# Storing L in halves, sharing its tiles between short steps, packing the last pair's right sides, and loading two weight pieces apart

## The chip, the cores and the metric

One core of a Trainium2 chip runs the whole program: TensorE (PE) multiplies, VectorE (DVE) and ScalarE (ACT) do elementwise work, SyncE (SP) issues most transfers and ACT the rest. The metric is the device time of one execution in microseconds; less is better.

## The reference

```python
# attention: 8 x 8 heads, 576 positions of 64, in two steps through 32 packed rows
p_packed = sm_attn(p, k, v)
x = sm_attn(q, p_packed, p_packed)          # as 4608 tokens x 512
# first block
a = x @ w1; b = x @ w2                      # 512 -> 1024
x = (a * b @ w3) @ w_out                    # -> 512
# second block
h = x @ w_in                                # 512 -> 2048
g = where(h >= 1, h, where(h <= -1, 0.0, (h + 1) ** 2 / 4))
return g @ w_out                            # -> 512
```

Everything is float32.

## The kernel before, in words

Attention and the first block fill the first 588 us. They leave x, transposed, in DRAM. The change touches what follows, the second block.

**Products.** A float32 factor is split into a high part and a rest, and a product is three passes: high times high, high times rest, rest times high. Both layers of the second block use a scheme with seven products of half blocks instead of eight. Its products are named A11, S1, S2, A12, S4, S3 and A22; each has its weights (`wi` tiles, or `ws` tiles for S4 and A22, the two in `STREAM`, which are loaded anew for each step) and its right side (`x2s` tiles, made from x by `x2_tasks`).

**Steps.** The first layer (line 999) has 40 steps `s`. The tokens go in five pairs of column blocks (`PAIRS`): four wide pairs of 2 x 512 tokens and a short one of 2 x 256. A pair has eight steps `i`, one for each 128 rows of a quarter of the weights. A step issues its products in the order A11, S1, S2, then A22 of the step before, then A12, S4, S3, six matrix products each (two row halves times three passes). They collect in three PSUM banks: A11, S2, S3 and A22 in x, S1 and S4 in z, A12 in y.

**What follows a product.** ACT copies the first sums out (`m1`, `m5`, `u2`, line 879). DVE adds them to later ones (line 883) and so makes the four quarters of h: two in a U tile, two in an L tile. The last of these adds, `L<-x,m`, reads bank x after S3; only then may A22 go on in that bank. The activation is three ACT instructions (816, 819) and a DVE one (822) for each quarter. `upper` treats U; `lower_begin`, `lower_relu` and `lower_middle` treat L, after A22. `upper_end` (849) and `lower_end` (872) form three differences in the third plane of U and the last two of L. Of U's three planes two are stored, in single pieces; of L's four planes (G21, G22, GT3, GT2) all, in one transfer of 1 MB (512 KB in the short pair). Stores are gathered in a list and issued by SP at the end of a step (`flush_stores`, 833). U and L have two tiles each, so a step's first write into a tile waits until the store of two steps before has landed.

**Right sides.** While a pair runs, `x2_tasks` makes the seven right sides of the next one, eleven tasks, dealt out over the steps by the tables `MID` and `LAST`. A task `parts` is one ACT instruction (678) and one DVE instruction (679); a task `combine` one DVE instruction (673). There are nine `x2s` tiles, so the third right side of the next pair takes the tile of this pair's A11, which is free only in step 7.

**Near the end of the layer** `first_sides` loads the first weights (`w`, `hwi`) and inputs (`raw`) of the second layer, through SP too. The second layer (line 1093) reads the stored planes back as `raw` or `r`, splits them into `op` tiles (967, 968) and multiplies (1102).

**Queues.** SP and ACT each issue their instructions in order. A transfer's landing is told by one of eight counters, which the program gives out in turn over both queues; a transfer that gets a counter first waits until the counter's previous transfer has landed.

Of the kernel before, what the change touches and what calls it, by code (L numbers as in the profile page):

```python
# [56 lines left out]
def fused_kernel(ctx: ExitStack, tc, qT, kT, vv, pb, w1, w2, w3T, wo, win, wout, out):  # L57
# [610 lines left out]
    def x2_tasks(t):  # L668

        N = PAIRS[t][1]  # L670

        def combine(dst, a, b):
            return lambda: nc.vector.tensor_tensor(out=x2f[dst], in0=x2f[a], in1=x2f[b], op=ALU.subtract)

        def parts(q, src):
            def f():
                x = x2_t[t, q] = late["b1"].tile([P, 2, 2, 512], F32R, name="x2s", tag="x2s", bufs=9)
                nc.scalar.activation(out=x[:, 0, :, :N], in_=x2f[src], func=AF.Copy)
                nc.vector.tensor_tensor(  # L679
                    out=x[:, 1, :, :N], in0=x2f[src], in1=x[:, 0, :, :N].bitcast(F32), op=ALU.subtract)  # L680
            return f
        return [
            parts(A11, 11), combine(11, 12, 11), combine(12, 22, 12), parts(S1, 11), combine(11, 22, 11),
            parts(S2, 11), parts(A12, 21), parts(S4, 22), parts(S3, 12), combine(11, 21, 11), parts(A22, 11),
        ]
# [66 lines left out]
    def ws_tile():  # L752
        return wp.tile([P, 2, 2, 2, P], F32R, name="ws", tag="ws", bufs=2)

    def ws_load(s, eng):
        if s < 8 * len(PAIRS):
            t = ws_t[s] = first.pop("ws", None) or ws_tile()
            eng.dma_start(out=t.bitcast(F32), in_=wst[s % 8 // 4][:, s % 4])
# [13 lines left out]
    first["ws"] = ws_tile()  # L772
# [5 lines left out]
    ws_load(0, nc.sync)  # L778
    for i in (S2, A12, S3):
        wi_load(i, 0)  # L780
    ws_load(1, nc.sync)
# [12 lines left out]
    def product(s, q):  # L794
# [7 lines left out]
        for k in range(2):  # L802
            for v, m in PASSES:
                if q in STREAM:
                    w = ws_t[s][:, STREAM.index(q), k, v, :]
# [55 lines left out]
    def lower_middle(s):  # L861
# [5 lines left out]
        smaller(h[:, 1, :N], h[:, 1, :N], r[:, 1])  # L867

    def lower_end(s):
# [5 lines left out]
        store(s, G21, 4, h[:, :, :N])  # L875
# [98 lines left out]
    LAST = {2: 2, 3: 1, 4: 1, 5: 1, 7: 2, 0: 1}  # L974

# [23 lines left out]
    for s in range(steps):  # L999
# [19 lines left out]
        if s:  # L1019
            product(s - 1, A22)  # L1020
            ws_load(s + 1, nc.scalar)
            lower_relu(s - 1)
            lower_middle(s - 1)
# [6 lines left out]
        tasks(MID.get(i, 0))  # L1030
        kept[s, 1] = buf("L")
        product(s, S4)
        add(kept[s, 0][:, 1, :N], bank.pop((s, "z")), u2, N)
        product(s, S3)
        add(kept[s, 1][:, 1, :N], bank[s, "x"], m5, N)
        tasks(LAST.get(i, 0))
        if s and not short:
            if i == 0:
                upper_end(s - 1)
            lower_end(s - 1)  # L1040
        flush_stores()
# [136 lines left out]
```

## Time and profile before

| | |
|---|---|
| median of 3 runs (lowest to highest) | 1317.23 us (1315.96 to 1319.09) |
| the profiled execution | 1317.88 us, its span 1316.1 us |
| PE busy | 1260.2 us, 96% |
| DVE busy | 878.0 us, 67% |
| ACT busy | 677.1 us, 51% |
| mean granted TensorE clock | 0.993 |
| DMA | 299.46 MB, mean 228 GB/s |

A share of 96% does not say that 4% is all there is to win: a product that waits in the middle of a group counts partly as busy, and the share is a mean over stages with different limits. The span is the profiler's; the device time has about 1.8 us more around it.

### The profile page before, as it was taken

Reading aid. Unit: us, or ns where it says so; the run is one execution under the profiler, and the core shown is the slowest. Engines: PE = TensorE matmul, PEld = TensorE weight load, DVE = VectorE, ACT = ScalarE, POOL = GpSimd, SP = SyncE. Lnnn points to the kernel's source line nnn. Section 1 sums busy time; section 2 is a strip of 40 time slices with the busy share of each in tenths; the row PEclk is TensorE's granted clock in tenths of the full one; section 3 lists DMA queues with packets and bytes.
Section 4 is the critical chain, followed back from the end, with each engine's and each line's share of the span. In section 5 each row is a group of like instructions: output and inputs, shape, how many; then the busy total and the mean of one; then the engine's idle time right before and its main releaser. Section 6 shows DMA issues by size and latency. Waiting matters only on the chain.

```text
span 1316.1 us, 21364 instructions
## 1 busy us (share of the span) xinstructions
PE 1260.2 (96%) x8312; PEld 1055.6 (80%) x8312; DVE 878.0 (67%) x1462; ACT 677.1 (51%) x1144; POOL 0.7 (0%) x6
## 2 busy tenths in 40 slices
PE   6989989999999999999999999998899999999998
PEld 2367788889888889997878877787877788888888
DVE  5975777778577768625778877877557646455464
ACT  3444344545445454525677666766557343434433
POOL 0000000000000000000000000000000000000000
PEclk9999999999999999999999999999999999999999
DMA  9771674637466542278667675766999957768675
GB/s 352 252 249 59 212 245 159 235 135 253 135 209 196 210 152 95 99 264 288 239 207 267 219 277 199 250 224 201 323 365 324 375 197 262 252 224 287 210 225 176
DMA packets 125397, 299.46 MB, mean 228 GB/s; under 512 B 10352, under 2 KB 53360, under 8 KB 120816
## 3 DMA queue, kind: packets, MB, share of 16 engines
q1 hardware_dynamic: 86352, 232.94, 50.7%
q10 hardware_dynamic: 38944, 65.16, 14.6%
q8 instruction: 65, 1.06, 0.4%
q14 instruction: 36, 0.29, 0.1%
HBM read 196.21 MB, written 101.84 MB: 226 GB/s over the span
## 4 chain that ended last, share of the span: by engine, by line
PE 63%; DVE 14%; DMA 14%; ACT 6%; issue 3%; ACTq 1%; SPq 0%; DVEq 0%
PE x L1102 13%; PE psk L405 12%; PE psk L381 9%; PE x L808 7%; PE z L1102 6%; DMA g<-L 6%; PE y L1102 4%; PE z L808 3%; PE psk L489 3%; PE y L808 2%; PE psk L181 2%; DMA wi<-hl 1%; DMA raw<-g 1%; DVE x2s L679 1%; DMA g<-U 1%
## 5 line engine op out<-in xcount | busy, mean ns | idle before, releaser
L381 PE MATMUL psk<-at,m 128*128 128x288 f32 x1494 | 213.1, 298 | 5.2 <-ACT ta L391 2.7
L405 PEld LDWEIGHTS psk<-g,w 128*128 128x128 f32 x1500 | 199.9, 188 | 20.4 <-ACT st L432 6.3
L381 PEld LDWEIGHTS psk<-at,m 128*128 128x128 f32 x1494 | 200.6, 188 | 17.8 <-issue 7.4
L405 PE MATMUL psk<-g,w 128*128 128x288 f32 x1500 | 206.2, 296 | 6.2 <-ACT st L432 2.8
L808 PE MATMUL x<-x2s,wi 128*128 128x512 f32 (+1 forms) x720 | 163.8, 372 | 2.9 <-ACT m L879 2.9
L808 PEld LDWEIGHTS x<-x2s,wi 128*128 128x128 f32 x720 | 127.0, 190 | 28.3 <-ACT m L879 4.6
L968 DVE TENSOR_TENSOR op<-raw,op 128x1024 fp32r<-128x1024 f32 (+1 forms) x94 | 101.8, 1114 | 69.5 <-ACT op L967 69.1
L967 ACT ACTIVATE op<-raw 128x1024 fp32r<-128x1024 f32 (+1 forms) x94 | 87.4, 966 | 70.9 <-DVE raw L959 32.5
L1102 PE MATMUL x<-op,w 128*128 128x512 f32 (+1 forms) x480 | 101.5, 371 | 1.4 <-DVE op L968 1.4
L1102 PE MATMUL x<-op,hwi 128*128 128x512 f32 (+1 forms) x480 | 100.9, 369 | 0.5 <-DVE op L968 0.5
L1102 PEld LDWEIGHTS x<-op,w 128*128 128x128 f32 x480 | 84.4, 190 | 17.8 <-DVE op L968 2.5
L1102 PEld LDWEIGHTS x<-op,hwi 128*128 128x128 f32 x480 | 82.9, 188 | 17.0 <-DVE op L968 1.3
L393 DVE TENSOR_TENSOR tb<-psk,ta 128x288 f32<-128x288 f32 x124 | 56.2, 453 | 57.8 <-ACT ta L391 36.0
L819 ACT ACTIVATE r<-r 128x1024 f32<-128x1024 f32 (+1 forms) x80 | 78.0, 975 | 2.5
L968 DVE TENSOR_TENSOR op<-r,op 128x1024 fp32r<-128x1024 f32 (+1 forms) x46 | 50.2, 1117 | 38.9 <-ACT op L967 38.7
L489 PE MATMUL psk<-wo,w3f 128*128 128x512 f32 x128 | 62.5, 641 | 11.6 <-DVE w3f L136 11.6
L879 ACT ACTIVATE m<-x 128x512 f32<-128x512 f32 (+1 forms) x40 | 22.1, 552 | 91.5 <-PE x L808 82.9
L125 ACT ACTIVATE cvt<-raw 128x512 f32<-128x512 f32 x72 | 48.3, 676 | 40.3 <-DMA raw<-w 10.7
L808 PE MATMUL x<-x2s,ws 128*128 128x512 f32 (+1 forms) x240 | 60.1, 384 | 9.3 <-DVE L L883 8.2
L391 ACT ACTIVATE ta<-psk 128x288 f32<-128x288 f32 x125 | 50.4, 403 | 28.3 <-PE psk L381 24.3
L967 ACT ACTIVATE op<-r 128x1024 fp32r<-128x1024 f32 (+1 forms) x46 | 43.2, 969 | 39.0 <-DVE L L1079 15.7
L489 PEld LDWEIGHTS psk<-wo,w3f 128*128 128x128 f32 x128 | 25.5, 207 | 44.1 <-issue 28.3
(118 smaller groups left out, 1898.7 us busy)
## 6 DMA issues: line engine op xcount, KB each, us to landing
raw<-g SPq DMA_DIRECT2D x86, 512.0 KB, 5.2
g<-L SPq DMA_DIRECT2D x32, 1024.0 KB, 6.3
r<-g SPq DMA_DIRECT2D x42, 512.0 KB, 5.2
ws<-ws ACTq DMA_DIRECT2D x38, 512.0 KB, 5.1
g<-U SPq DMA_DIRECT2D x64, 256.0 KB, 5.8
x2d<-st ACTq DMA_DIRECT2D x72, 144.0 KB, 2.1
v<-vv SPq DMA_DIRECT2D x8, 1280.0 KB, 7.3
wi<-hl ACTq DMA_DIRECT2D x20, 512.0 KB, 3.3
```

Source lines behind the costliest of these rows:

```text
L125: nc.scalar.activation(out=t, in_=raw.bitcast(F32).rearrange("p (n two) -> p n two", two=2)[:, :, 1], func=AF.Copy, scale=2.0 ** -112)
L181: nc.tensor.matmul(ps[r][NP * q:NP * q + NP], stat[64 * r:64 * r + 64, NP * q:NP * q + NP], mov(q)[64 * r:64 * r + 64], start=True, stop=True,
L381: nc.tensor.matmul(ps[w][:, :HS], m_tile[b, w, n][:, s, G, c0 * P:(c0 + 1) * P], at_tile[b][:, G, v, hf * HS:(hf + 1) * HS], start=(k == 0 ...
L391: nc.scalar.activation(out=bs, in_=ps[1][:, :HS], func=AF.Copy)
L393: nc.vector.tensor_tensor(out=g, in0=ps[0][:, :HS], in1=bs, op=ALU.mult)
L405: nc.tensor.matmul(ps, w34[kt][:, s, mt * P:(mt + 1) * P], g_t[kt, hf][:, v, :], start=(kt == kts[0] and n == 0), stop=(kt == kts[-1] and ...
L489: nc.tensor.matmul(acc[4 * hf + m], w3f[hf, j][:, m * P:(m + 1) * P], wof[j], start=(j == 0), stop=(j == 7))
L808: nc.tensor.matmul(bank[s, b][:, :N], w, x2_t[t, q][:, m, k, :N], start=(j == 0 and q in (A11, S1, A12)), stop=(j == 5), skip_group_check= ...
L819: nc.scalar.activation(out=r, in_=r, func=AF.Square)
L967: nc.scalar.activation(out=o[:, :, 0, :N], in_=a[0], func=AF.Copy)
L968: nc.vector.tensor_tensor(out=o[:, :, 1, :N], in0=a[0], in1=o[:, :, 0, :N].bitcast(F32), op=ALU.subtract)
L1102: nc.tensor.matmul(bank[b][d][:, :N], w2_t[q][j // 2][:, 2 * (j % 2) + k, s, d * P:(d + 1) * P], op[x][:, k, v, :N], start=start and k == ...
```

## The change

- `store`: L's first two planes (G21, G22) are stored when `lower_middle` has made them, and flushed there with U's stores; `lower_end` stores only the last two (GT3, GT2), named from GT3 on.
- L's tiles in the short pair: an even and an odd step share one tile of 512 columns.
- Right sides of the short pair: two share one `x2s` tile. While the fourth pair runs, its tasks are dealt out by `LAST_SHORT`, with none in the middle of a step.
- `lower_end` in step 7 of a pair goes ahead of the tasks.
- `ws`: one tile and load for S4's piece and one for A22's, 256 KB each instead of 512 KB for both. S4's is loaded by ACT two steps ahead, right after product S4; A22's by SP one step ahead, at the end of a step.

```diff
@@ -672,9 +672,19 @@
         def combine(dst, a, b):
             return lambda: nc.vector.tensor_tensor(out=x2f[dst], in0=x2f[a], in1=x2f[b], op=ALU.subtract)
 
+        room = []
+
         def parts(q, src):
             def f():
-                x = x2_t[t, q] = late["b1"].tile([P, 2, 2, 512], F32R, name="x2s", tag="x2s", bufs=9)
+                if not room:
+                    x = late["b1"].tile([P, 2, 2, 512], F32R, name="x2s", tag="x2s", bufs=9)
+                    if N == 512:
+                        room.append(x)
+                    else:
+                        x = x.rearrange("p a b (c n) -> p (a b c n)", n=N).rearrange(
+                            "p (o a b n) -> p o a b n", o=2, a=2, b=2)
+                        room.extend([x[:, 0], x[:, 1]])
+                x = x2_t[t, q] = room.pop(0)
                 nc.scalar.activation(out=x[:, 0, :, :N], in_=x2f[src], func=AF.Copy)
                 nc.vector.tensor_tensor(
                     out=x[:, 1, :, :N], in0=x2f[src], in1=x[:, 0, :, :N].bitcast(F32), op=ALU.subtract)
@@ -749,13 +759,13 @@
     def wi_load(i, n):
         nc.sync.dma_start(out=wi_t[i, n].bitcast(F32), in_=wid[i][n])
 
-    def ws_tile():
-        return wp.tile([P, 2, 2, 2, P], F32R, name="ws", tag="ws", bufs=2)
-
-    def ws_load(s, eng):
+    def ws_tile(x):
+        return wp.tile([P, 2, 2, P], F32R, name=f"ws{x}", tag=f"ws{x}", bufs=2)
+
+    def ws_load(s, x, eng):
         if s < 8 * len(PAIRS):
-            t = ws_t[s] = first.pop("ws", None) or ws_tile()
-            eng.dma_start(out=t.bitcast(F32), in_=wst[s % 8 // 4][:, s % 4])
+            t = ws_t[s, x] = first.pop(f"ws{x}", None) or ws_tile(x)
+            eng.dma_start(out=t.bitcast(F32), in_=wst[s % 8 // 4][:, s % 4, x])
 
 
     for tag in ("m1", "m5", "U", "u2"):
@@ -769,16 +779,18 @@
         wi_tile(i, 1, wp)
     for i in (S1, S2):
         wi_tile(i, 0, wp)
-    first["ws"] = ws_tile()
+    for x in range(2):
+        first[f"ws{x}"] = ws_tile(x)
     wi_tile(A12, 0, wq)
     wi_tile(S3, 0, wq)
     wi_tile(S3, 1, wo2)
     for i in (A11, S1):
         wi_load(i, 0)
-    ws_load(0, nc.sync)
+    ws_load(0, 0, nc.sync)
+    ws_load(0, 1, nc.sync)
     for i in (S2, A12, S3):
         wi_load(i, 0)
-    ws_load(1, nc.sync)
+    ws_load(1, 0, nc.sync)
 
 
     BANK = {A11: "x", S1: "z", A12: "y", S2: "x", S4: "z", S3: "x", A22: "x"}
@@ -802,7 +814,7 @@
         for k in range(2):
             for v, m in PASSES:
                 if q in STREAM:
-                    w = ws_t[s][:, STREAM.index(q), k, v, :]
+                    w = ws_t[s, STREAM.index(q)][:, k, v, :]
                 else:
                     w = wi_t[q, n][:, k, v, c0 * P:(c0 + 1) * P]
                 nc.tensor.matmul(
@@ -865,6 +877,8 @@
         square(r)
         smaller(h[:, 0, :N], ps, r[:, 0])
         smaller(h[:, 1, :N], h[:, 1, :N], r[:, 1])
+        store(s, G21, 2, h[:, :2, :N])
+        flush_stores()
 
     def lower_end(s):
         N = PAIRS[s // 8][1]
@@ -872,7 +886,7 @@
         nc.vector.tensor_tensor(
             out=h[:, 2:4, :N], in0=h[:, 1:2, :N].to_broadcast([P, 2, N]), in1=kept.pop((s, 0))[:, 1:3, :N],
             op=ALU.subtract)
-        store(s, G21, 4, h[:, :, :N])
+        store(s, GT3, 2, h[:, 2:4, :N])
 
     def copy(tag, ps, N):
         c = buf(tag)[:, :N]
@@ -972,6 +986,7 @@
 
     MID = {7: 1, 0: 1}
     LAST = {2: 2, 3: 1, 4: 1, 5: 1, 7: 2, 0: 1}
+    LAST_SHORT = {2: 2, 3: 2, 4: 1, 5: 1, 6: 1, 7: 2, 0: 1}
 
 
     def first_sides(s):
@@ -1018,7 +1033,6 @@
         u2 = copy("u2", bank[s, "x"], N)
         if s:
             product(s - 1, A22)
-            ws_load(s + 1, nc.scalar)
             lower_relu(s - 1)
             lower_middle(s - 1)
         product(s, A12)
@@ -1027,17 +1041,27 @@
         short = t + 1 == len(PAIRS) and i
         if short:
             lower_end(s - 1)
-        tasks(MID.get(i, 0))
-        kept[s, 1] = buf("L")
+        to_short = t + (i > 0) + 1 == len(PAIRS)
+        tasks(0 if to_short else MID.get(i, 0))
+        if t + 1 < len(PAIRS):
+            kept[s, 1] = buf("L")
+        else:
+            if s % 2 == 0:
+                both = buf("L")
+            kept[s, 1] = both[:, :, s % 2 * N:(s % 2 + 1) * N]
         product(s, S4)
+        ws_load(s + 2, 0, nc.scalar)
         add(kept[s, 0][:, 1, :N], bank.pop((s, "z")), u2, N)
         product(s, S3)
         add(kept[s, 1][:, 1, :N], bank[s, "x"], m5, N)
-        tasks(LAST.get(i, 0))
-        if s and not short:
+        if i == 7 and not short:
+            lower_end(s - 1)
+        tasks((LAST_SHORT if to_short else LAST).get(i, 0))
+        if s and i < 7 and not short:
             if i == 0:
                 upper_end(s - 1)
             lower_end(s - 1)
+        ws_load(s + 1, 1, nc.sync)
         flush_stores()
         for w in {0: (A11, S1), 1: (S2, A12, S3)}.get(s, ()):
             wi_load(w, 1)
```

The first place is SP's queue where the first layer begins: the loads for step 0 and 1, before the stores of step 0. `wi` with a number is one product's weights, in the order A11, S1, S2, A12, S3 for the first five; DMAHW0 to DMAHW7 are the eight counters. Before:

```order
L750 DMA wi_7300<-wi_60 128x2048 [waits DMAHW2_49,PE_49]
L750 DMA wi_7308<-wi_62 128x2048 [waits DMAHW3_49,PE_49]
L758 DMA ws<-ws_74 128x1024 [waits DMAHW4_49]
L750 DMA wi_7309<-wi_64 128x2048 [waits DMAHW5_49]
L750 DMA wi_7311<-wi_66 128x2048 [waits DMAHW7_49,DMAHW6_49]
L750 DMA wi_7312<-wi_70 128x2048 [waits DMAHW7_49,PE_49]
L758 DMA ws<-ws_74 128x1024 [waits DMAHW0_49]
L750 DMA wi_7301<-wi_61 128x2048 [waits DMAHW1_49]
```

and now:

```order
L760 DMA wi_7300<-wi_60 128x2048 [waits DMAHW2_49,PE_49]
L760 DMA wi_7308<-wi_62 128x2048 [waits DMAHW3_49,PE_49]
L768 DMA ws_7310<-ws_74 128x512 [waits DMAHW4_49]
L768 DMA ws_7311<-ws_74 128x512 [waits DMAHW5_49]
L760 DMA wi_7309<-wi_64 128x2048 [waits DMAHW6_49]
L760 DMA wi_7312<-wi_66 128x2048 [waits DMAHW7_49]
L760 DMA wi_7313<-wi_70 128x2048 [waits DMAHW0_49,PE_49]
L768 DMA ws_7322<-ws_74 128x512 [waits DMAHW1_49]
L768 DMA ws_7371<-ws_74 128x512 [waits DMAHW2_49]
```

The load for S3, the fifth `wi`, moved from counter 7 to counter 0, and the loads behind it one on as well.

The second place is the same queue in the short pair, where step 36 and the first stores of step 37 stand. `U` and `L` rows are stores, `w` and `raw` are loads for the second layer. Before:

```order
L833 DMA g_87<-U 128x256 [waits DMAHW1_49,DVE_49]
L833 DMA g_87<-U 128x256 [waits DMAHW2_49,DVE_49]
L833 DMA g_87<-L 128x4x256 [waits DMAHW3_49,DVE_49]
L917 DMA w_9919<-w_76 128x512 [waits DMAHW4_49]
L950 DMA raw_10150<-g_83 128x1024 [waits DMAHW5_49,PE_49]
L833 DMA g_87<-U 128x256 [waits DMAHW7_49,DVE_49]
L833 DMA g_87<-U 128x256 [waits DMAHW0_49,DVE_49]
```

and now:

```order
L845 DMA g_87<-U 128x256 [waits DMAHW1_49,DVE_49]
L845 DMA g_87<-U 128x256 [waits DMAHW2_49,DVE_49]
L845 DMA g_87<-L 128x2x256 [waits DMAHW4_49,DVE_49]
L768 DMA ws_10251<-ws_75 128x512 [waits DMAHW5_49,PE_49]
L845 DMA g_87<-L 128x2x256 [waits DMAHW6_49,DVE_49]
L931 DMA w_10020<-w_76 128x512 [waits DMAHW7_49]
L964 DMA raw_10259<-g_83 128x1024 [waits DMAHW0_49]
L845 DMA g_87<-U 128x256 [waits DMAHW2_49,DVE_49]
L845 DMA g_87<-U 128x256 [waits DMAHW3_49,DVE_49]
```

A step has seven transfers on SP where it had five; with ACT's one `ws` load these are eight and six. The second `L` row of a step is the half that `lower_end` makes.

The third place is DVE in the short pair, from the middle of step 32's activation to the add that ends step 33. `L<-x,m` is that add, the one that A22 waits for. Before:

```order
L822 SCALAR_TENSOR_TENSOR U<-U,r 128x256
L849 TENSOR_TENSOR U<-U 128x256 [waits DVE_49]
L822 SCALAR_TENSOR_TENSOR L<-x,r 128x256 [waits Activation_49]
L822 SCALAR_TENSOR_TENSOR L<-L,r 128x256
L883 TENSOR_TENSOR U<-y,m_9852 128x256 [waits DMAHW7_49,DMAHW6_49,PE_49]
L872 TENSOR_TENSOR L<-L,U 128x2x256 [waits DVE_49]
L883 TENSOR_TENSOR U<-z,u_9877 128x256 [waits PE_49]
L883 TENSOR_TENSOR L<-x,m_9869 128x256 [waits DMAHW0_49,PE_49]
```

and now:

```order
L834 SCALAR_TENSOR_TENSOR U<-U,r 128x256
L861 TENSOR_TENSOR U<-U 128x256 [waits DVE_49]
L834 SCALAR_TENSOR_TENSOR L<-x,r 128x256 [waits Activation_49]
L834 SCALAR_TENSOR_TENSOR L<-L,r 128x256
L897 TENSOR_TENSOR U<-y,m_9951 128x256 [waits DMAHW6_49,DMAHW2_49,PE_49]
L886 TENSOR_TENSOR L<-L,U 128x2x256 [waits DVE_49]
L897 TENSOR_TENSOR U<-z,u_9976 128x256 [waits PE_49]
L897 TENSOR_TENSOR L<-x,m_9968 128x256 [waits PE_49]
```

The order of these rows is the same; the add has lost its wait for counter 0, since step 33 writes into the tile that step 32 took.

## Rows read from the trace of the kernel before

**Rows 1.** The chain that ended last, shares by engine.
```profile
PE 63%; DVE 14%; DMA 14%; ACT 6%; issue 3%; ACTq 1%; SPq 0%; DVEq 0%
```

**Rows 2.** That chain by time: start, duration, what; 740 to 890 us.
```profile
747.89 2.35 DVE x2s L679 x2
...
751.40 7.00 DMA g<-L
...
771.55 8.48 DMA g<-L
...
878.18 2.75 PE x L808 x12
```

**Rows 3.** Waits: total, times, longest; 588 to 904, then 904 to 962.
```profile
DVE L L883 <- DMA g<-L: 32.0, 16, 3.2
...
DVE L L883 <- DMA g<-L: 7.5, 3, 3.8
```

**Rows 4.** PE's timeline: start, duration, tile, count; 586 to 985 us.
```profile
589.85 1.54 PE L808 MATMUL z<-x2s,wi 128*128 128x512 f32 x6
...
904.82 0.86 PE L808 MATMUL z<-x2s,wi 128*128 128x256 f32 x6
...
946.72 0.87 PE L808 MATMUL z<-x2s,wi 128*128 128x256 f32 x6
947.42 0.90 PE L808 MATMUL x<-x2s,wi 128*128 128x256 f32 x6
...
962.02 11.94 PE L1102 MATMUL x<-op,w 128*128 128x512 f32 x48
```

**Rows 5.** Windows: busy times, then granted clock, DMA's busy share, GB/s.
```profile
904.10:920.00 15.90, 12.00 (x76) 10.84 (x75) 12.64 (x23) 10.03 (x18) 0.00 (x0) 0.88 0.45 146
920.00:962.00 42.00, 35.53 (x269) 34.16 (x269) 25.49 (x63) 24.77 (x52) 0.00 (x0) 0.95 0.98 326
962.00:1000.00 38.00, 37.36 (x159) 29.70 (x158) 23.08 (x27) 22.99 (x32) 0.00 (x0) 0.98 0.99 346
```

**Rows 6.** Transfers issued from 904 to 962: count, KB, median us to landing.
```profile
g<-L SPq DMA_DIRECT2D x7, 512.0 KB, 5.6
g<-L SPq DMA_DIRECT2D x2, 1024.0 KB, 7.1
...
g<-U SPq DMA_DIRECT2D x14, 128.0 KB, 6.9
```

**Rows 7.** SP's waits and timeline, 570 to 600, and PE's first S3.
```profile
SPq L758 <- DMA x2d<-st: 9.9, 2, 9.5
...
594.45 0.32 SPq L758 DMA_DIRECT2D ws<-ws  x1
...
596.03 3.00 PE L808 MATMUL x<-x2s,wi 128*128 128x512 f32 x12
```

**Rows 8.** PE and DVE's timeline in the short pair; in brackets the idle time before.
```profile
912.76 0.42 DVE L883 TENSOR_TENSOR U<-z,u 128x256 f32<-128x256 f32 x1
...
913.83 0.98 PE L808 MATMUL x<-x2s,wi 128*128 128x256 f32 x6 [2.15 <-ACT m L879]
...
916.36 2.04 PE L808 MATMUL x<-x2s,ws 128*128 128x256 f32 x6 [1.55 <-DVE L L883]
...
951.80 0.94 PE L808 MATMUL z<-x2s,ws 128*128 128x256 f32 x6 [2.06 <-DMA ws<-ws]
...
952.39 0.43 DVE L883 TENSOR_TENSOR U<-y,m 128x256 f32<-128x256 f32 x1 [0.60 <-DMA g<-U]
...
960.57 1.65 PE L808 MATMUL x<-x2s,ws 128*128 128x256 f32 x6 [2.14 <-DVE L L883]
```

**Rows 9.** SP's waits from 904 to 962.1.
```profile
SPq L833 <- DMA raw<-g: 3.1, 2, 2.1
```

**Rows 10.** The chain that ended last, 962 to 1000 us.
```profile
970.15 10.63 DMA raw<-g
...
988.88 8.49 PE x L1102 x35
```

## The prediction, made before the changed kernel was run

> **What bounds the kernel now.** I read the chain that ended last first: matrix products hold 63% of the span, and DVE and DMA share 14% each [rows 1]. The chain by time then shows where the DMA share sits in the stage that the change touches (588 to 962 us): pieces named "DMA g<-L" of 7 to 8.5 us, each the store of an L tile that a later step wants back [rows 2]. The waits say what stands behind them: DVE's add into L (line 883) sat 32.0 us in 16 waits for that store in the four wide pairs, and 7.5 us in 3 waits in the short pair [rows 3]. PE feels it, because the product A22 goes into the bank that this add must first read.
>
> How much PE loses comes from starts. Twelve matrix products take 2.75 us [rows 2], so one group of six takes 1.375; from S1 of step 0 at 589.85 to S1 of step 32 at 904.82 there are 222 wide groups and a narrow one, 305.9 us, and 315.0 passed: 9.0 us lost in the wide pairs [rows 4]. A narrow group takes 947.42 - 946.72 = 0.70 [rows 4]; from 904.82 to the last stage's first product at 962.02 stand one wide and 55 narrow groups, 39.9 us, and 57.2 passed: 17.3 us lost in the short pair. So 26 us is all that this stage can give.
>
> The windows add the other limit: DMA was busy 0.45 of the time from 904 to 920, then 0.98 to 962 and 0.99 to 1000 [rows 5]. Work that gets faster there meets transfers that do not.
>
> **The sum, against the profiled execution.** It took 1317.88 us (span 1316.1 and 1.8 around it), 0.65 over the median of the runs, 1317.23; I subtract from the median, since the terms are differences.
>
> *L in halves, wide pairs: -6.0.* G21 and G22 leave about half a step earlier; what the add waits for is the second half, issued where the whole tile was, but 512 KB. The nearest rows are those of the short pair: an L of 512 KB landed after 5.6 us, one of 1024 KB after 7.1 [rows 6]. That is 1.5 us per wait directly, and more in a row of waits, since a late add makes the next store late ([rows 2]: the store issued at 751.40, with the right-side work of 747.89 ahead of it, led to the one at 771.55). At step 7 of a pair the change also puts lower_end ahead of that right-side work, 2.35 us earlier for two DVE instructions [rows 2]. The upper bound is the whole 9.0. From the rows: PE lost 9.0 for 32.0 waited, 0.28 of each; 16 waits shorter by 1.5 are 24 us, times 0.28 is 6.7. Some of the 9.0 is right-side work at a pair's border, which stays. The lower bound, 3.0, is that half as many waits are long enough to matter. I take 6.0.
>
> *The start: +1.2.* The order of SP's queue shows that cutting the first ws load in two moves every later load to the next counter. The load for S3, which had counter 7, now has counter 0, where the store of an x2 piece was pending: the ws load that stood there waited 9.5 us, until 594.45, while S3's first product began at 596.03 [rows 7]. A 1 MB load issued at 594.45 cannot be there at 596.03. With S3's megabyte out of the way the store should land one to two us sooner, and the load takes some 4 to 5 us; the stall is 0 to 3.0, and I take 1.2. The loads queued behind it are used a step later or more.
>
> *The short pair: -8.3.* (a) Step 32's z sum into U ran at 912.76, 0.42 long, so its add into L could have ended at 913.6; A22 began at 916.36 [rows 8]. The add waited for step 30's store, whose second half now leaves ahead of the border's right-side work and is half as large: -2.7. (b) The other two waits of the 7.5 [rows 3] are 4.8 us. Odd short steps wait for no store of L any more, as the order shows, and even ones for stores two steps older; DVE has slack for part of the wait, so -2.0. (c) Granted clock was 0.88 of full from 904 to 920 and 0.95 from 920 to 962 [rows 5], 1.9 and 2.1 us lost if PE had been busy throughout: a stretch at the lower level, 1.2 GHz, right after the idle 2.15 and 1.55 us of [rows 8]. With those two idles shortened I expect most of it back; at three quarters busy, -2.9 (bounds 0 and -4.0). (d) ws of S4 is now loaded two steps ahead. The wait of 2.06 at 951.80 goes; but U's y sum waited for its own store until 952.39 [rows 8], just as late, so I count three quarters of it, -1.5. (e) Right sides packed by twos need four tiles instead of seven, so A12's no longer waits for step 31; no instruction is added, and what it saves lies in the DVE work ahead of the add, which (a) already counts. (f) Each short step from 36 on issues eight transfers instead of six, and there are eight counters. SP already stood 3.1 us for a counter whose load had not landed [rows 9]: +0.8. The wait at the end, 2.14 before A22 at 960.57 [rows 8], is a chain of DVE work with no next step to cover it, and stays.
>
> *The last stage: +2.0.* Its first products are gated by loads: one was 10.63 us under way, and PE stood at 988.88 [rows 10]. DMA was full from 920. If it is filled from 904 on, those loads can come earlier by at most 0.55 x 15.9 + 0.02 x 42 = 9.6 us [rows 5]; the early short steps can't issue that much, so I take two thirds, 6.3. What PE gained beyond that, 8.3 - 6.3, is given back (bounds 0 and 4).
>
> Edits at no cost: A22's ws piece on SP stands where PE's use of the old one is a step past; on ACT the S4 load waits for product S4, when ACT's next work needs the product after it anyhow. If a counter is late there, ACT's copy m1 and then PE's S2 wait.
>
> Sum: -6.0 + 1.2 - 8.3 + 2.0 = **-11.1**, from 1317.2 to **1306.1 us**.
>
> **A rule against it.** The three kinds of store in [rows 6] were under way 7 x 5.6 + 2 x 7.1 + 14 x 6.9 = 150 us inside 58: they overlap, so a transfer's fixed part is not paid by its neighbours. The stretch with mostly small ones ran at 326 GB/s, the next one at 346 with DMA as full [rows 5]; size cost 6%. The Trainium skill, "DMA: Bandwidth & Descriptors", section "Bandwidth", says to batch transfers to 1 MiB or more for 75% of peak, and a section before it gives each some 2 us of fixed time (fitted on another issue path than this kernel's). Sixteen extra transfers in the short pair paid one after another would be 32 us, an estimate from that page, and the kernel would be slower; by the rows they are not.
>
> **Rivals.**
> 1. *No give-back.* The early loads keep up, or more of the wide pairs' 9.0 is L's (7.0): 1306.1 - 2.0 - 1.0 = 1303. For it: 9.6 us of free DMA time; against: it is free only before most of the loads can be issued. Chance 0.15.
> 2. *Counters bind.* With eight transfers a step and 6.9 us to land [rows 6], a step from 36 on takes about 7 us, not 5: four steps, +8, and the short pair gives nothing; the last stage takes nothing back. -6.0 + 1.2 = -4.8: 1312.4. For it: [rows 9]; against: halves land sooner. Chance 0.20.
> 3. *Smaller transfers slow the DMA* by another 6% where it is full: 42 x 0.06 = 2.5 us, 1308.6. Chance 0.07. This is the rule of the Trainium skill's page as far as the rows bear it out.
> 4. *Slower: ACT stuck on a counter in the wide pairs.* The S4 load is now in front of ACT's next copy m1 and takes a counter last used eight transfers, 1.3 steps or 12.8 us, before. If that one lands later than this, PE's S2 waits in every step. It decides from 11.1/32 = 0.35 us a step on; at 0.8 us it is +14: 1332. The rows have landings of 5.6 to 10.6 us [rows 6, 10], so it needs rare ones to be common. Chance 0.05.
> 5. *No effect:* the add still waits, for the later half lands as late as the whole did: 1317. Chance 0.03.
>
> The forecast has 0.50. **Range and chances.** The term bounds give -18 (wide 7.5, start 0, short 10.5, last 0) to -3 (wide 3, start 3, short 4, last 1); rivals 1 to 3 lie inside. I leave out the slow case and the last corner: 1300 to 1313. A change of 0.2% (2.6 us) is about what can be told from none. Faster 0.87, the same 0.07 (rival 5 and the weak end of 2), slower 0.06.
>
> **What would show it.** "DVE L <- DMA g<-L" should fall from 32.0 us to under 8 in the wide pairs and go in the short one; S1 of step 0 to S1 of step 32 to about 310 us; S1 of step 32 to the last stage's first product from 57.2 to about 49; no stretch at the lower clock there; a new wait of PE for the wi load in step 0 before S3 of about a microsecond; more idle time of PE before the op tiles between 950 and 990. I am wrong if SP's waits for landed transfers grow by more than about 8 us in the short pair, or if DVE's wait moves from L's stores to U's.

## The result, and the profile after

| | before | changed |
|---|---|---|
| median of 6 runs (lowest to highest) | 1317.06 us (1315.21 to 1321.07) | 1303.00 us (1299.80 to 1307.11) |
| ratio to before, 95% interval | | 0.989 (0.9868 to 0.9913) |
| the profiled execution, its span | 1317.88, 1316.1 | 1304.39, 1302.6 |

The changed kernel is 14.1 us faster by the medians and 13.5 by the profiled executions; the forecast was 11.1.

The chain that ended last, by engine; DVE and DMA had 14% each in [rows 1]:

```profile
PE 69%; DVE 10%; DMA 10%; ACT 7%; issue 2%; ACTq 1%; SPq 0%; DVEq 0%
```

DVE's waits in the wide pairs (588 to 900 us: total, times, longest). The add into L is now line 897; it waited 32.0 us in 16 waits in [rows 3], and now:

```profile
DVE L L897 <- DMA g<-L: 3.9, 2, 2.0
```

In the short pair, where it waited 7.5 us, the view has no such row any more.

PE's timeline at the places of [rows 4], and the last waits of the short pair, which answer to [rows 8]:

```profile
592.63 0.85 PE L820 MATMUL z<-x2s,wi 128*128 128x512 f32 x3
...
597.75 0.73 PE L820 MATMUL y<-x2s,wi 128*128 128x512 f32 x2 [2.21 <-DMA wi<-wi]
...
902.06 0.84 PE L820 MATMUL z<-x2s,wi 128*128 128x256 f32 x6
...
909.79 0.97 PE L820 MATMUL x<-x2s,wi 128*128 128x256 f32 x6 [0.98 <-ACT m L893]
...
948.52 1.27 PE L820 MATMUL x<-x2s,ws 128*128 128x256 f32 x6 [2.01 <-DVE L L897]
949.59 1.05 PE L1126 MATMUL x<-op,w 128*128 128x512 f32 x2
```

From S1 of step 0 (592.63) to S1 of step 32 (902.06) it is 309.4 us, where 315.0 passed before; from there to the last stage's first product 47.5, where it was 57.2. Of the waits of [rows 8] that of S2 is 0.98 in place of 2.15, those of A22 (1.55) and S4 (2.06) are gone, the one at the end stays, 2.01 for 2.14. A new one of 2.21 stands in step 0, before A12.

Windows of the short pair and the start of the last stage (granted clock, DMA's busy share and GB/s are the last three columns), against 0.88, 0.95 and 0.98 and 146, 326 and 346 GB/s in [rows 5]:

```profile
901.00:917.00 16.00, 14.97 (x115) 14.02 (x114) 13.76 (x27) 11.98 (x23) 0.00 (x0) 1.00 0.83 274
917.00:950.00 33.00, 30.47 (x234) 28.82 (x233) 22.67 (x57) 22.95 (x49) 0.00 (x0) 0.98 1.01 346
950.00:990.00 40.00, 39.91 (x170) 32.25 (x169) 25.88 (x31) 25.70 (x36) 0.00 (x0) 0.97 1.03 369
```

Transfers issued from 900 to 990 (count, KB, median us to landing), against 5.6 to 7.1 us from 904 to 962 in [rows 6] (in the changed kernel's short pair alone, 902 to 949.6, both medians are 4.4):

```profile
g<-L SPq DMA_DIRECT2D x16, 256.0 KB, 4.5
...
g<-U SPq DMA_DIRECT2D x16, 128.0 KB, 4.5
```

For the experiments I read the same four places in each profile: S1 of step 0, S1 of step 32, the first product of the last stage, the end of the span. The columns "wide pairs" and "short pair" of the table are the times between the first three; what each kernel is stands with its experiment below. The code ahead of the first is the same everywhere, yet it lay between 588.4 and 594.2 us: from 49 to 147 us the granted clock was 0.98 in the profile before and 0.95 in the one after. So the lengths tell more than the spans. "Products 0 to 10" is from the last stage's first product to that of its twelfth op tile. Each ratio is to runs of the kernel before taken together with that kernel's, and need not be the quotient of the medians.

| kernel | S1 of step 0 | wide pairs | short pair | products 0 to 10 | median us, ratio to before (interval) |
|---|---|---|---|---|---|
| before | 589.85 | 315.0 | 57.2 | 32.4 | 1317.06 |
| changed | 592.63 | 309.4 | 47.5 | 31.9 | 1303.00, 0.9890 (0.9868 to 0.9913) |
| h_alone | 592.70 | 307.4 | 53.0 | 31.4 | 1306.96, 0.9923 (0.9907 to 0.9939) |
| no_h | 590.66 | 310.5 | 48.8 | 32.5 | 1304.70, 0.9903 (0.9887 to 0.9920) |
| no_end7 | 592.10 | 308.6 | 47.3 | 32.1 | 1304.75, 0.9910 (0.9882 to 0.9938) |
| no_h_end7 | 590.03 | 311.5 | 48.7 | 32.0 | 1304.67, 0.9909 (0.9879 to 0.9939) |
| ws_late | 589.88 | 310.7 | 55.7 | 31.7 | 1308.39, 0.9915 (0.9883 to 0.9947) |
| ws_on_sp | 592.11 | 318.7 | 51.3 | 31.9 | 1314.07, 0.9975 (0.9957 to 0.9993) |
| no_share | 594.15 | 309.3 | 47.3 | 32.0 | 1304.51, 0.9896 (0.9868 to 0.9924) |
| no_pack | 592.83 | 308.2 | 48.0 | 31.9 | 1305.40, 0.9901 (0.9875 to 0.9927) |
| quarters | 590.00 | 308.9 | 50.8 | 36.1 | 1308.72, 0.9939 (0.9918 to 0.9959) |
| start | 591.29 | 307.0 | 47.7 | 31.6 | 1302.18, 0.9885 (0.9869 to 0.9902) |
| start2 | 588.42 | 307.0 | 47.3 | 32.8 | 1300.55, 0.9880 (0.9863 to 0.9896) |
| best_m2 | 593.73 | 308.4 | 47.6 | 31.6 | 1302.82, 0.9884 (0.9854 to 0.9914) |

Without any idle time the wide pairs take 305.9 by the prediction's own count.

### The profile page after: what moved, and what is told of

Read it like the earlier page. It is cut to its first block, busy times and chain, and to the rows that moved or that the text cites. A ratio compares the mean times of both kernels' runs of the same rounds, so it can differ in the third digit from the quotient of the medians.

```text
span 1302.6 us, 21560 instructions
## 1 busy us (share of the span) xinstructions
PE 1254.8 (96%) x8312; PEld 1055.4 (81%) x8312; DVE 876.9 (67%) x1462; ACT 674.0 (52%) x1144; POOL 0.7 (0%) x6
## 4 chain that ended last, share of the span: by engine, by line
PE 69%; DVE 10%; DMA 10%; ACT 7%; issue 2%; ACTq 1%; SPq 0%; DVEq 0%
PE x L1126 14%; PE psk L405 12%; PE x L820 11%; PE psk L381 9%; PE z L1126 6%; PE z L820 6%; PE y L1126 4%; PE y L820 3%; DMA raw<-w 2%; DMA wi<-hl 2%; PE psk L181 2%; DMA x2d<-st 1%; ACT r L828 1%; ACT r L831 1%; DVE tb L393 1%
## 5 line engine op out<-in xcount | busy, mean ns | idle before, releaser
L981 ACT ACTIVATE op<-raw 128x1024 fp32r<-128x1024 f32 (+1 forms) x94 | 87.3, 966 | 71.0 <-DVE raw L973 32.4
L834 DVE SCALAR_TENSOR_TENSOR U<-U,r 128x512 f32<-128x512 f32 (+1 forms) x80 | 47.4, 633 | 37.3 <-ACT r L831 37.3
L104 ACT ACTIVATE g<-tb 128x288 fp32r<-128x288 f32 x128 | 56.2, 439 | 7.7 <-DVE tb L393 7.1
```

Of the source, the lines that this page charges most:

```text
L104: nc.scalar.activation(out=dst[:, 0], in_=src, func=AF.Copy)
L981: nc.scalar.activation(out=o[:, :, 0, :N], in_=a[0], func=AF.Copy)
```

## The experiments

### Are the halves what freed the wide pairs?

My theory was the prediction's: the half is smaller and lands sooner. First the halves alone on the kernel before, then everything but the halves. Edit of h_alone (no_h undoes the same lines in the changed kernel):

```diff
 lower_middle:
+        store(s, G21, 2, h[:, :2, :N])
+        flush_stores()
 lower_end:
-        store(s, G21, 4, h[:, :, :N])
+        store(s, GT3, 2, h[:, 2:4, :N])
```

> The kernel before with one part of the change alone: L is stored in halves, the first as soon as G21 and G22 are ready; nothing else differs. Theory (the halves carry the wide pairs): the loss of the wide pairs falls from 8.6 us to about 2, DVE's wait for L's stores there from 32 us to under 8, and step 32's wait shrinks too (2 to 3 us); the rest of the short pair stays: 1307 to 1309, against 1317.1 of the kernel before and 1303.0 of the changed one. Rival (the gain of the wide pairs comes from the earlier ws pieces or from lower_end at step 7): at most 3 us faster, 1314 or more, with DVE's wait for L still above 15 us.

> The changed kernel with L stored whole again, the other parts kept. Theory: the loss of the wide pairs is back at 7 to 9 us, and shared tiles alone keep some 5 to 7 us of the short pair's gain: 1311 to 1314. Rival (halves hardly matter, or only with packing): within 2 us of the changed kernel, 1303 to 1305. If the short pair alone loses more than 4 us, the halves matter there as well as the shared tiles.

h_alone came out as the theory has it: 1306.96 us, and DVE's wait in the wide pairs (588 to 900) is

```profile
DVE L L885 <- DMA g<-L: 5.9, 3, 2.4
```

But no_h missed it: with L stored whole the wide pairs lost only 1.1 us of their gain (1.9 with step 0's stalls left out on both sides), and the short pair 1.3. In the wide pairs the halves are enough, and they aren't needed. The next two asked whether the earlier lower_end at step 7 is the other cure. Edit of no_end7 (no_h_end7 has it on top of no_h):

```diff
-        if i == 7 and not short:
-            lower_end(s - 1)
         tasks((LAST_SHORT if to_short else LAST).get(i, 0))
-        if s and i < 7 and not short:
+        if s and not short:
```

> The changed kernel, but at step 7 of a pair the last DVE work and store of L stand behind the right-side work again, as in the kernel before; L in halves and the rest kept. Theory (halves and the earlier place at step 7 are two cures of one wait, each enough for most of it): the wide pairs lose at most 1 us more than the changed kernel, DVE's wait for L's stores stays under 8 us: 1303 to 1304.5. Rival (the two add up): the waits behind the pairs' borders are back, 2 to 3 us: 1305 to 1306.

> The changed kernel with L stored whole and, at step 7 of a pair, with L's last DVE work behind the right-side work: both of the parts that touch L's stores in the wide pairs undone. Theory (these two are what freed the wide pairs, one for the other): the wide pairs lose some 8 us again, as before, and DVE's wait for L's stores there is above 20 us: 1307.5 to 1310. Rival (a third part did it, the ws pieces, which no longer load on ACT in the middle of a step): the loss stays at 3 to 4 us: 1304 to 1306.

It isn't. no_end7, which has the halves, keeps the wait at 3.5 us and the wide pairs at 308.6. no_h_end7 has neither of the two parts and 1304.67 us; the theory for it, over 20 us of waiting for L's stores, falls:

```profile
DVE L L895 <- DMA g<-L: 6.0, 7, 1.6
```

Of its 5.6 us over the bare 305.9, 4.3 lie in steps 0 and 1: S3 waited 2.2 us for its wi load there, and products behind it ran at the lower clock (steps 0 and 1 took 11.15 and 10.97 us; bare they take 8.25 and 9.61). In the first three pairs one part of the change is left in this kernel: ws in two pieces, S4's from ACT behind product S4, some 8.4 us into the step, A22's from SP. (In the fourth pair the right-side tasks are placed anew as well.) In those three pairs alone the wait for L's stores fell from 28.2 us in 14 waits to 5.9 in 7.

### The ws load and L's store

The trace of before shows the two together. DVE's, SP's and ACT's pieces at one place:

```profile
690.62 0.69 DVE L883 TENSOR_TENSOR L<-x,m 128x512 f32<-128x512 f32 x1 [2.61 <-DMA g<-L]
691.23 1.22 DVE L872 TENSOR_TENSOR L<-L,U 128x1024 f32<-128x1024 f32 x1
...
692.47 0.37 SPq L833 DMA_DIRECT2D g<-L  x1
...
693.06 0.35 ACTq L758 DMA_DIRECT2D ws<-ws  x1
```

The add that waited 2.61 us for the store of L of two steps earlier is followed by lower_end of the step between (1.22) and its store, at 692.47; the 512 KB of ws leave on ACT's queue 0.6 us later, and U's two stores behind them. Two edits of the kernel before move this load and cut nothing. ws_late:

```diff
         if s:
             product(s - 1, A22)
-            ws_load(s + 1, nc.scalar)
 ...
         product(s, S4)
+        if s:
+            ws_load(s + 1, nc.scalar)
```

and ws_on_sp:

```diff
-            ws_load(s + 1, nc.scalar)
+            ws_load(s + 1, nc.sync)
```

> The kernel before with one edit: the whole load of ws, 512 KB, stays on ACT but is issued behind product S4 instead of in front of ACT's relu of L, some 2 to 3 us later in each step; L is stored whole, nothing is cut. Theory (in the kernel before this load and L's store start within 0.1 us of each other and share the transfers, the store is late, so the next add and the next store too; moving the load out from beside it is enough): DVE's wait for L's stores in the wide pairs falls from 32 to 12 us or less, L's store is issued 1 to 2 us earlier in the step, 1309 to 1312. Rival (it takes smaller pieces, not another place): the wait stays above 25 us, 1316 to 1318.

> The kernel before with one edit: the whole load of ws is issued by SP at the same place of the program, not by ACT, so that ACT's relu of L has nothing in front of it, while the load still goes out just before L's store. Theory (the transfers side by side are what delays the store): DVE's wait for L's stores stays above 20 us, 1314 to 1318. Rival (the 0.35 us of issue on ACT and the 0.33 us behind it delay L's relu, and so its store): the wait falls below 15 us, 1308 to 1312.

ws_late is 8.5 us faster by the medians, a little more than the theory had, and 7.0 by the spans, 4.2 of them in the wide pairs and 1.5 in the short pair. Its wait (588 to 900) is what the theory said, 12 or less:

```profile
DVE L L883 <- DMA g<-L: 11.6, 8, 2.5
```

ws_on_sp answered neither way, since its premise was wrong: on SP's queue the load does not go out ahead of L's store but behind it, for SP issues in order. The wait for L's stores was gone (the rival's number), the time was 1314.07 (the theory's number), and the reason is a third one, PE's wait for ws (both 588 to 900):

```profile
DVE L L883 <- DMA g<-L: 0.2, 1, 0.2
...
PE z L808 <- DMA ws<-ws: 6.8, 3, 2.7
```

The issue times and landings show the mechanism. Each pair is when a transfer was issued and when it had landed, in us from its step's first product, worked out from SP's and ACT's queues and from landings in the traces; around the border at step 8:

```
step   before: L, ws              ws_late: L, ws             ws_on_sp: L, ws
 9   8.64-15.48,  8.28-12.75    5.67-10.72, 7.22-16.14    5.71-10.79, 6.80-18.71
10   5.22-13.33,  5.81-12.40    2.78-13.30, 6.50-12.69    2.86-12.80, 5.69-14.06
11   7.94-12.47,  6.12- 9.81    8.03-13.49, 6.94-10.91    4.49- 9.54, 5.89-12.15
12   5.51-11.58,  5.69-10.28    6.44-12.25, 6.68-11.35    3.35- 7.74, 5.69-10.02
13   5.04- 9.46,  5.69-12.02    5.52- 9.93, 6.57-12.50    3.35- 7.74, 5.69-10.09
14   3.66- 8.03,  5.69-11.95    3.40- 7.56, 6.56-12.11    3.36- 7.75, 5.69-11.44
```

In before, a store that left with ws or up to 0.6 us behind it landed after 6.1 to 8.5 us; one that left 0.6 us or more ahead of it after 4.2 to 4.8, but for steps 2, 3, 10 and 18, where 1 to 2 MB of wi or f were under way too (so step 10 is slow in all three columns); two that left 1.8 us behind it (steps 11 and 19) took 4.5 and 4.8. And lateness hands itself on: the next step's store leaves when this one has landed, plus 0.69 and 1.22 of DVE, and some 1.2 for a right-side piece where the step has one. In before, from step 12 to 13: 5.51 + 6.06 - 9.61 + 1.91 + 1.2 = 5.07, and the trace has 5.04; from step 4 (10.24 long) to 5: 6.86 + 6.28 - 10.24 + 1.91 + 1.2 = 6.01, and the trace has 5.98. So in such a step the store must land within 9.61 - 3.1 = 6.5 us, or the next one is no earlier. The right-side work and the load of f at a border make one store late, the late one meets ws, which leaves 5.7 us into the step, and it stays late (steps 8 to 13 here). In ws_late step 9 is freed, but the store that f delayed in step 10 is followed by late ones until step 13, as before; in ws_on_sp the store is back in time at step 12.

On ACT's queue ws overtakes: in step 10 of ws_late it left 3.7 us after the store and landed before it; on SP's it landed after it every time. The Trainium skill, "DMA: Bandwidth & Descriptors", section "Queues, rings and completion order", says that a DMA engine with work from several queues takes packets from them in turn, while one queue's descriptors are consumed in order; these rows agree. The price of SP's queue is what stands in it: behind the loads of wi (step 2) and of f (steps 9 and 17) ws landed 18.7 to 19.4 us after the step began, and S4 of the next step had to wait, 6.8 us in three times.

ws_late and ws_on_sp both also take 0.35 us of issue away from in front of ACT's relu, so these two runs don't separate that from the moved transfer. The rows say that its part is small: at step 28, where nothing waits, L's store leaves at 3.11 us in before and at 2.83 in ws_late; at step 16 it leaves at 5.92 and 5.63 and lands after 7.00 and 4.84. And h_alone, which leaves this issue where it was, ends most of the waiting too. That smaller or moved transfers end most of the waiting is shown four ways (halves, pieces, later, behind).

### The parts of the short pair

no_share gives each short step an L tile again; no_pack gives every right side of the short pair its own tile, and LAST and MID as before:

```diff
 no_share:
-        if t + 1 < len(PAIRS):
-            kept[s, 1] = buf("L")
-        else:
-            if s % 2 == 0:
-                both = buf("L")
-            kept[s, 1] = both[:, :, s % 2 * N:(s % 2 + 1) * N]
+        kept[s, 1] = buf("L")
 no_pack:
-                if not room:
+                if True:
 ...
-                    if N == 512:
+                    if True:
 ...
-    LAST_SHORT = {2: 2, 3: 2, 4: 1, 5: 1, 6: 1, 7: 2, 0: 1}
+    LAST_SHORT = {2: 2, 3: 1, 4: 1, 5: 1, 7: 2, 0: 1}
-        tasks(0 if to_short else MID.get(i, 0))
+        tasks(MID.get(i, 0))
```

> The changed kernel, but each short step has an L tile of its own again (two in turn); the rest kept. Theory (short steps come so fast that an L tile is wanted back before its store has landed; landings there are 4.5 us, a step 5.5): DVE's adds wait for L's stores in most short steps, A22 stalls 0.5 to 1.5 us in some: 2 to 4 us slower than the changed kernel, 1305 to 1307. Rival (halves that land after 4.5 us are soon enough, and step 32's wait was all): within 1 us of it, 1303 to 1304.

> The changed kernel with every right side of the short pair in a tile of its own again and the right-side tasks placed as in the kernel before; halves, shared L tiles and ws pieces kept. Theory (packing lets the short pair's right sides be made earlier than their wide tiles come free; without it DVE's and ACT's right-side work stands in steps 32 to 34): the two short waits of the kernel before at step 33 and 34, 1 and 1.7 us, are back: 2 to 4 us slower than the changed kernel, 1305 to 1307. Rival (packing saves nothing, as the prediction had it): within 1 us, 1302.5 to 1304.

Sharing is worth nothing that can be seen: 47.3 us for the short pair without it, 47.5 with it, and DVE's wait there (901 to 950) is

```profile
DVE L L897 <- DMA g<-L: 0.4, 1, 0.4
```

Packing is worth about half a microsecond of the short pair (48.0). PE's timeline of no_pack has the wait of step 33's S2 as it was before, 2.05 in place of 0.98, and steps 34 to 38 are as short as in the changed kernel:

```profile
909.78 0.97 PE L820 MATMUL x<-x2s,wi 128*128 128x256 f32 x6 [2.05 <-ACT m L893]
```

By the medians neither is told from the changed kernel. Of the 9.7 us of the short pair h_alone (halves alone) has 4.2 and ws_late 1.5; no_h_end7 (whole stores, ws in pieces, with sharing and packing) has 8.5. So most of it needs no halves, and with the halves and the pieces there sharing adds nothing. What sharing does for whole stores no run shows, since in the changed kernel it was taken out only beside the halves; the 9.7 can't be split further.

### Do counters or small transfers bind?

quarters cuts the short pair's L stores once more, the second half (GT3) like the first: ten transfers a step, where the changed kernel has eight.

```diff
-        store(s, G21, 2, h[:, :2, :N])
+        if N == 512:
+            store(s, G21, 2, h[:, :2, :N])
+        else:
+            store(s, G21, 1, h[:, :1, :N])
+            store(s, G21 + 1, 1, h[:, 1:2, :N])
```

> The changed kernel, but in the short pair each store of L is cut once more, into four transfers of 128 KB a step: ten transfers a step on eight counters, the suspected cost of the counters and of small transfers made larger. Rival 2 of the prediction (counters bind at eight a step): with ten a step every step from 36 on is held to about 10/8 of 4.5 us, 5.6 us or more, SP's waits for landed transfers above 10 us, 1305 to 1310. Rival 3 (small transfers slow DMA): the windows from 917 to 990 move less than 330 GB/s and the last stage starts to wait: 1305. Theory (a transfer of 128 KB lands in some 4 us whatever its size beside others, so neither binds yet): within 1 us, 1302.5 to 1304.

At ten a step something binds: 5.7 us slower than the changed kernel by the medians; in the profiles the short pair takes 3.3 more and products 0 to 10 of the last stage 4.2. SP's waits from 917 to 950, for transfers landed (counters) first, then its queue:

```profile
SPq L845 <- DMA w<-w: 3.9, 3, 2.4
...
SPq L939 <- DMA ws<-ws: 1.6, 2, 1.0
SPq L845 <- DMA raw<-g: 1.2, 1, 1.2
```

```profile
930.25 3.36 SPq L845 DMA_DIRECT2D g<-L  x2
933.67 0.42 SPq L939 DMA_DIRECT2D w<-w  x1
934.13 0.46 SPq L972 DMA_DIRECT2D raw<-g  x1
934.69 0.86 SPq L845 DMA_DIRECT2D g<-U  x2
935.64 1.40 SPq L845 DMA_DIRECT2D g<-L  x2
937.13 1.24 SPq L768 DMA_DIRECT2D ws<-ws  x1
938.46 1.97 SPq L845 DMA_DIRECT2D g<-L  x2
940.48 1.27 SPq L939 DMA_DIRECT2D w<-w  x1
```

The rows of L with 3.36 and 1.97 us hold two of these waits, 2.4 for a load of w and 1.2 for one of raw; the rest of the stretch is mostly issuing, a median of 0.43 us for each transfer and up to 1.27, so from 930 to 942 SP's queue had hardly a gap. From 917 to 950 its waits for landed transfers come to 7.2 us, below the 10 that were set for rival 2; with the changed kernel's eight transfers a step they came to 1.9 (1.0 for ws, 0.9 for raw). S2 of steps 38 and 39 waited for ACT's copy (1.29 and 1.24), the copy for DVE's first add into U, and that for U's store of two steps before:

```profile
934.18 0.42 DVE L905 TENSOR_TENSOR U<-y,m 128x256 f32<-128x256 f32 x1 [1.39 <-DMA g<-U]
```

This store had left SP 1.7 us later, counted from S1 of step 32, than in the changed kernel (28.7 for 27.0), and it landed after 6.5 us in place of 4.0. So the queue and the transfers both had a part. DMA moved less:

```profile
917.00:950.00 33.00, 27.25 (x210) 25.29 (x208) 20.21 (x50) 20.66 (x44) 0.00 (x0) 1.00 0.93 288
950.00:990.00 40.00, 36.96 (x151) 29.19 (x151) 22.27 (x26) 22.13 (x30) 0.00 (x0) 0.96 1.01 371
```

288 GB/s against 346 to 950, and 371 against 369 behind it. So what rivals 2 and 3 of the prediction describe is seen two transfers a step further on, but not apart: part of the 288 is SP standing, and the run prices neither the counters, nor SP's issuing, nor small transfers by themselves.

### The start

start moves one line, start2 two:

```diff
-    ws_load(0, 0, nc.sync)
-    ws_load(0, 1, nc.sync)
     for i in (S2, A12, S3):
         wi_load(i, 0)
+    ws_load(0, 0, nc.sync)
+    ws_load(0, 1, nc.sync)
```

(start leaves the first of them where it was.)

> The changed kernel, but the load of A22's first ws piece is issued after the loads of S2, A12 and S3, so that these three get the counters that they had in the kernel before. Theory (the stall of 2.37 us in step 0 is A12's load waiting for the counter of an x2 store that landed at 592.7): A12's load leaves some 7 us earlier and PE's wait for it is under 0.8 us; S3 takes the counter that A12 had and may still stall up to 1 us; 1.2 to 2 us faster than the changed kernel, 1301 to 1302. Rival (transfers are full at that time, so that an earlier place only exchanges which load is late): within 0.7 us of 1303, with the stall moved to S3 or to S2.

> The changed kernel, but both first ws pieces are issued after the loads of S2, A12 and S3, which so get counters whose x2 stores land by 585. Theory (counters): no product of step 0 waits over 0.5 us for a wi load, S4's ws piece takes the late counter and, at 256 KB, lands within 3 us of it, before 596.5: 2 to 2.5 us faster than the changed kernel, 1300.5 to 1301. Rival (transfers): three loads of 1 MB under way together land no earlier than 593 to 596, and the stall stays 1 to 2 us at A12 or goes to S4's piece: 1302 to 1303.

Both take away the whole of step 0's wait: its six groups take 8.25 us in each, 10.75 in the changed kernel, and the wide pairs 307.0 in place of 309.4. The theory (counters) holds; transfers were not too full. SP's queue in the changed kernel, where it took 8.42 us to get three wi loads out because the second, A12's, waited for its counter until 592.7, and in start2:

```profile
585.12 8.42 SPq L760 DMA_DIRECT2D wi<-wi  x3
593.66 1.08 SPq L768 DMA_DIRECT2D ws<-ws  x2
```

```profile
575.73 7.87 SPq L760 DMA_DIRECT2D wi<-wi  x3
586.81 5.39 SPq L768 DMA_DIRECT2D ws<-ws  x4
```

In start2 the three are out by 583.6. It has the lowest median here, 1300.55. By stages it beats the changed kernel by the 2.4 us of step 0; by the ratios alone the two can't be told apart.

best_m2 adds a second m1 tile to start2:

```diff
-    "u2": ([P, 512], 1), "r": ([P, 2, 512], 2), "m1": ([P, 512], 1), "m5": ([P, 512], 1),
+    "u2": ([P, 512], 1), "r": ([P, 2, 512], 2), "m1": ([P, 512], 2), "m5": ([P, 512], 1),
 ...
-    hp.tile([P, 544], F32, name="gap", tag="gap", bufs=1)
+    hp.tile([P, 32], F32, name="gap", tag="gap", bufs=1)
```

> The changed kernel with the load order of start2 (both first ws pieces behind the loads of S2, A12 and S3) and two tiles in turn for m1 in place of one (the room comes from an unused gap of 2 KB beside them). Theory (in the short pair ACT's copy m1 waits 1.2 to 1.6 us for the DVE add that reads the one m1 tile, and PE's S2 of step 33 waits 1.14 us for that copy): this wait goes, the short pair takes 1 to 1.5 us less: 1299 to 1300 against 1300.5 of start2. Rival (the copy then waits for the bank instead, or the time is lost at the loads of the last stage): within 0.7 us of start2.

The rival had it: S2 of step 33 no longer waits, but A22 behind it does, about 0.4 us for DVE's add, and the step takes 6.16 us for 6.20 in start2, the short pair 47.6 for 47.3.

## Why the prediction was right, and where its sizes were off

The sum of the profiles is +2.8 before the stage (the clock of an earlier stage), -5.5 in the wide pairs and the start, -9.7 in the short pair and -1.1 behind it: -13.5. The prediction had -4.8, -8.3 and +2.0 for the last three. From the start of the first layer on the change thus gave 16.3 us in these two profiles, where 11.1 was forecast; that the total came nearer than that is luck, the 2.8 us that the profile after lost before the changed code.

**L in halves, wide pairs, -6.0.** Apart from step 0 the wide pairs gained 7.2 (the stall at the start took 1.7 of it back; 5.5 net). The wait that was named is the one that went, 32.0 to 3.9, below the 8 that was set. What was wrong is to whom the gain was put down: the ws pieces stood among the edits at no cost, and without the halves they take the wait from 32.0 to 6.0. Either part is enough; the prediction asked only how fast half a store lands and not what else lands beside it.

**The start, +1.2.** It cost 1.7 against before (step 0: 10.75 for 9.03), inside the bounds, but at another load: I followed S3's to counter 0 and not A12's, one counter on as well, to the one of an x2 store that landed at 592.73. A12 is used first. S3's load didn't stall.

**The short pair, -8.3.** -9.7. (a) and (b), L's waits: gone, and beside the halves without sharing too. (c) The clock is 1.00 and 0.98 where it was 0.88 and 0.95, as expected. (d) S4's wait for ws is gone, and DVE's waits for U's stores came to 0.7 in the whole layer, where they were 2.8. (e) Packing at nothing: about -0.5. (f) Counters at +0.8: SP's waits for landed transfers came to 1.9 and no product waited for them; landings had become shorter, 4.5 for 6.9. The end wait stayed, 2.01.

**The last stage, +2.0.** This step failed. Products 0 to 10 took 31.9 for 32.4, so nothing was given back. The prediction took it that these products had no slack against their loads, but in the kernel before PE waited there for op tiles only 0.5 us in all (962 to 995), and how much earlier the loads could be needed was not asked. And DMA ran at 274 GB/s in the short pair's first 16 us where it had 146, 2.0 MB more, and the early loads kept up. That is rival 1, with more of the wide pairs; that its 1303 is the measured time is in part chance, by the 2.8 above. The limit is near: start2 came to this stage at full clock, waited 1.9 us for op tiles and took 32.8; the changed kernel's first products ran at the lower clock behind the 2.01 us wait (granted 0.76 from 950 to 955), which gave the loads time. That this is why it waited less is read from these two, not tried.

**The rule against it** (batching to 1 MiB or more, the Trainium skill, "DMA: Bandwidth & Descriptors", section "Bandwidth") did not decide: with twice as many stores of L, from 600 to 900, they landed after a median of 3.8 us for 6.1, U's after 2.2 for 5.8 (in h_alone, where this cut stands alone, after 3.2 and 4.3). At ten transfers a step in the short pair the window moved 288 GB/s for 346, with SP's waits in it.

**Slower by ACT's counter** (rival 4): nothing of it came. PE's S2 waits in the wide pairs at steps 9, 17 and 25 alone, 0.3 us each, and it did so before, 0.4; it decides from 0.35 in every step.

## What to carry to other kernels

A transfer's landing time depends on what leaves beside it: before cutting or speeding up a store that is waited for, look which loads other queues issue within the same microseconds, and move those. Where a buffer's store, its next use and the next store form a ring, write down the period less the work in it; a landing above that keeps itself late, and any one of several small moves ends it, so their gains don't add. One more transfer ahead of others moves each of them to the next counter: go through all that follow, the first used first, or put the new one last.

## What the runs showed of the hardware

A stall of PE cost more than itself in some places. ws_on_sp's step 3 has a wait of 2.15 us and took 4.0 more than its neighbours; granted clock around it:

```profile
620.00:627.00 7.00, 5.24 (x23) 3.94 (x21) 5.87 (x8) 5.69 (x8) 0.00 (x0) 1.00 1.00 370
627.00:632.00 5.00, 4.61 (x13) 3.69 (x14) 1.46 (x3) 0.00 (x0) 0.00 (x0) 0.66 0.85 334
632.00:640.00 8.00, 8.00 (x36) 6.55 (x35) 5.54 (x7) 6.54 (x9) 0.00 (x0) 1.00 0.53 171
```

Products there came at 0.43 us, as at 1.2 GHz, and at 0.23 before and after. The wait of 2.21 in step 0 of the changed kernel had no such stretch behind it (granted 1.00 from 597.7 to 606). In best_m2 steps 1 to 7 took 9.80 us each where other kernels have 9.61, every product 0.233 us after the last in place of 0.229, with the granted clock shown as 1.00 throughout; the same stood in steps 1 and 2 of ws_late. That is 1.3 us in best_m2; what it was stays open.
